# Weight loads of the -k rows issued from GpSimd's queue, those of the +k rows from SyncE's

## Chip, cores and metric

The kernel runs on one core of one Trainium2 chip. The metric is the device time of one execution in microseconds (us); lower is better. "Before" is the kernel without the change, "after" the kernel with it. Each execution is marked fast or slow: slow when it took over 1.5% longer than the fastest of the same kernel. Medians are over all executions.

## The reference

Two spectral filters work on the same input, and a gate mixes their results:

```python
x = A_x                                            # 1 x 2048 x 1024, bf16
g = sigmoid((x * gate_w).sum(-1, keepdims=True))
def branch(w_r, w_i):                              # w_r, w_i: 2048 x 513, bf16
    return irfft2(rfft2(x.astype(float32)) * (w_r + 1j * w_i), s=(2048, 1024)).astype(bfloat16)
a, b = branch(A_w_r, A_w_i), branch(B_w_r, B_w_i)
return g * a + (1 - g) * b
```

The weights are two groups, A and B, each of 2 x 2048 rows of 513 numbers: 1026 bytes a row, 4.2 MB a group. The +k rows are one half of each group, the -k rows the half that mirrors it in frequency.

## The kernel before

The transforms are matrix products on TensorE (PE), which leave their results in a buffer, PSUM. The other data lie in an on-chip memory of 128 rows, called partitions. ScalarE (ACT) and VectorE (DVE) copy the results out of PSUM, and VectorE also multiplies the spectrum by the weights. SyncE (SP) issues the loads (DMAs) in its own queue; GpSimd (POOL) has nearly nothing to do. A small scheduler in the kernel keeps each engine's operations in program order and works out the waits from keys that each operation says it reads or writes.

```python
def op(self, eng, fns, reads=(), writes=(), dma=False):
    ...
    for k in reads:
        o.deps |= self.writer[k]            # wait for who wrote it
    for k in writes:
        o.deps |= self.writer.get(k, set())   # wait for the earlier writer
        o.deps |= self.readers.get(k, set())  # and for everybody who reads it
    for k in reads:
        self.readers.setdefault(k, set()).add(o)
    for k in writes:
        self.writer[k] = {o}
        self.readers[k] = set()
    ...

def dma(eng, pairs, reads, writes, kind=True):
    S.op(eng, [lambda e, d=d, s=s: e.dma_start(d, s) for d, s in pairs], reads, writes, dma=kind)
```

The weight loads. `R5` holds group A, and `R2` holds group B. Partition 0 of `R2` first serves the gate, under the keys `zrow` and `gwt`:

```python
def wload(b):
    prs = []
    T = WR[b]; P = pit[id(T)]
    for pm in range(2):                       # +k rows, then -k rows
        for ii in range(4):
            for c in range(2):                # real, imaginary
                src = wsrc[b][c]; n = src.shape[-1]
                def part(r0, step, k0, k1):   # partitions 4*pm + ii, + 8, + 16, ...
                    prs.append((AP(T, (4*pm + ii)*P + (2*k0 + c)*NS, [[8*P, 16], [2*NS, k1-k0], [1, n]]),
                                AP(src.tensor, src.offset + r0*n, [[128*n, 16], [step*n, k1-k0], [1, n]])))
                ...
    dma("sp", prs, [], [("W", b)] + (["zrow", "gwt"] if b else []))
wload(0)
...                                           # wload(1) follows later, after stage_d(0)
```

`prod` is VectorE's product. `stage_i1` starts the inverse transform, and its copy out of PSUM writes `V` into `R1`, the buffer in which the input `x` lay (`allx` is the list of the 16 keys of `x`):

```python
def prod(b, m):
    r = [("X", 2*m), ("X", 2*m + 1), ("W", b)]          # two spectrum tiles and the weights
    dve(1230, tt(...), r, ["t0"])
    ...
def stage_i1(b, kg):
    ...
    w = [("V", b, kg)]
    if kg == 0:
        w += allx if b == 0 else [("W", 0)]
    ev(1024, ap(VR[b], kg*8, ...), pslot(s, 0, ...), [("ps", s)], w)
```

## Time and profile before

| | before |
|---|---|
| time | 163.45 us median of 2 runs (162.85 to 164.06) |
| profiled span | 159.0 us |
| PE, DVE, ACT busy | 78%, 76%, 77% |
| group A landed | 44.49 us (completion of its semaphore in the trace) |
| group B landed | 68.46 us |

The first line of the page gives busy time and share of the span; the chain line tells what the longest chain of waits ran through.

```profile
PE 124.6 (78%) x1015; PEld 90.0 (57%) x1024; DVE 120.4 (76%) x193; ACT 121.7 (77%) x132; POOL 0.2 (0%) x4
...
ACT 37%; PE 27%; DVE 22%; issue 7%; DMA 4%; SPq 1%; DVEq 0%
PE PS L313 27%; ACT R L302 21%; ACT RING L302 13%; DVE RING L316 12%; DVE R L316 6%; DMA R<-in_A_x_dram 4%; DVE RING L304 4%; ACT GROW L564 1%; ACT L564 1%; ACT V L302 1%; SPq L319 1%; DVEq L213 0%
```

No engine is full, so the chain has to be read stage by stage. This is the list of waits (who waited for whom: total us, times, longest us):

```profile
ACT R L302 <- PE PS L313: 20.9, 17, 5.1
...
DVE RING L316 <- DMA R<-in_A_w_i_dram: 10.2, 1, 10.2
```

VectorE stood 10.2 us for the weights of group A. Its timeline (start us, length us, what, elements, count, idle before and what ended it) shows when:

```profile
34.20 0.17 DVE L316 TENSOR_TENSOR ZG<-PS,GS 128x16 bf16<-128x16 f32 x1 [6.77 <-PE PS L313]
44.59 2.36 DVE L316 TENSOR_TENSOR RING<-R 128x2048 bf16<-128x2048 bf16 x2 [10.21 <-DMA R<-in_A_w_i_dram]
```

PE used up the work that it could do without that product, and then stood too; its next group of matmuls comes 3.1 us late. The profile found no releaser and calls it issue; these `KI` matmuls read the product, and VectorE's adds for it end at 48.2 us (46.87 + 1.29 in its timeline).

```profile
44.32 0.84 PE L313 MATMUL PS<-RING,S 128*128 128x512 bf16 x5 [0.34 <-ACT RING L302]
48.25 1.03 PE L313 MATMUL PS<-KI,RING 128*128 128x256 bf16 x8 [3.10 <-issue]
...
50.91 1.03 PE L313 MATMUL PS<-KI,RING 128*128 128x256 bf16 x8
...
54.62 1.04 PE L313 MATMUL PS<-DM,R 128*128 128x256 bf16 x8
```

How fast the weights came is in the windows view (stretch, its length, busy us of each engine with its number of instructions, granted TensorE clock, DMA share, GB/s):

```profile
22.00:32.00 10.00, 7.74 (x70) 4.28 (x70) 5.36 (x9) 8.35 (x10) 0.00 (x0) 1.00 1.14 171
```

The rate is 171 GB/s with the DMA engines full, while the page's slices show over 400 for the loads of `x` just before.

### The profile page before, as it was taken

The numbers are of one execution on the slowest core, as the hardware profiler recorded it, in microseconds if no ns is written. First come the engines' busy times: TensorE is split into PE (matmuls) and PEld (weight loads), VectorE is DVE, ScalarE is ACT, GpSimd is POOL, SyncE is SP. The second block draws the span as 40 slices with busy tenths as digits, with TensorE's granted clock in tenths as the row PEclk, the third lists the DMA queues.
The fourth block names the chain that finished last, engine by engine and source line by source line (L and its number), as shares of the span: only waits on it lengthen the run. The fifth ranks groups of instructions, "written<-read, shape, count | busy, mean of one in ns | idle before, by whom it ended". The sixth has DMA issues, their size and how long they took to land.

```text
span 159.0 us, 2541 instructions
## 1 busy us (share of the span) xinstructions
PE 124.6 (78%) x1015; PEld 90.0 (57%) x1024; DVE 120.4 (76%) x193; ACT 121.7 (77%) x132; POOL 0.2 (0%) x4
## 2 busy tenths in 40 slices
PE   0255897888928999999954999959999899898930
PEld 0244654355616767776633788847778576565600
DVE  0699998000079997998999999969923788989892
ACT  3045889629985988989955599999999499888850
POOL 0000000000000000000000000000000000000000
PEclk9999999999999999999995599999999999999995
DMA  5899999999999999950000000000000034243333
GB/s 168 296 429 415 257 168 167 177 167 165 179 168 170 181 169 169 197 191 4 0 0 0 0 5 0 0 0 4 0 0 1 4 112 152 86 180 123 145 132 132
DMA packets 13165, 19.53 MB, mean 123 GB/s; under 512 B 1505, under 2 KB 9825, under 8 KB 12770
## 3 DMA queue, kind: packets, MB, share of 16 engines
q1 hardware_dynamic: 13008, 19.37, 53.5%
q8 instruction: 8, 0.13, 0.4%
q14 instruction: 3, 0.02, 0.1%
q10 hardware_dynamic: 146, 0.00, 0.0%
HBM read 15.17 MB, written 4.19 MB: 122 GB/s over the span
## 4 chain that ended last, share of the span: by engine, by line
ACT 37%; PE 27%; DVE 22%; issue 7%; DMA 4%; SPq 1%; DVEq 0%
PE PS L313 27%; ACT R L302 21%; ACT RING L302 13%; DVE RING L316 12%; DVE R L316 6%; DMA R<-in_A_x_dram 4%; DVE RING L304 4%; ACT GROW L564 1%; ACT L564 1%; ACT V L302 1%; SPq L319 1%; DVEq L213 0%
## 5 line engine op out<-in xcount | busy, mean ns | idle before, releaser
L302 ACT ACTIVATE R<-PS 128x1024 bf16<-128x1024 f32 (+1 forms) x80 | 75.9, 1041 | 20.9 <-PE PS L313 20.9
L316 DVE TENSOR_TENSOR RING<-R 128x2048 bf16<-128x2048 bf16 (+1 forms) x48 | 48.0, 1041 | 16.9 <-DMA R<-in_A_w_i_dram 10.2
L302 ACT ACTIVATE RING<-PS 128x1024 bf16<-128x1024 f32 x40 | 42.8, 1135 | 8.0 <-PE PS L313 6.8
L316 DVE TENSOR_TENSOR RING<-RING 128x512 bf16<-128x512 bf16 (+1 forms) x96 | 44.6, 509 | 2.5 <-ACT RING L302 1.4
L313 PE MATMUL PS<-KI,RING 128*128 128x256 bf16 x256 | 34.0, 281 | 7.5 <-issue 3.1
L313 PE MATMUL PS<-DI,R 128*128 128x256 bf16 x256 | 32.7, 273 | 1.5 <-DVE RING L304 1.2
L313 PEld LDWEIGHTS PS<-KI,RING 128*128 128x128 bf16 x256 | 24.3, 101 | 14.0 <-issue 3.9
L313 PEld LDWEIGHTS PS<-DI,R 128*128 128x128 bf16 x256 | 24.4, 98 | 8.4 <-DVE RING L304 2.2
L313 PE MATMUL PS<-FM,R 128*128 128x128 bf16 x128 | 11.8, 266 | 13.0 <-DVE R L316 13.0
L313 PEld LDWEIGHTS PS<-FM,R 128*128 128x128 bf16 x128 | 10.1, 122 | 14.8 <-DVE R L316 14.4
L313 PE MATMUL PS<-RING,S 128*128 128x1 bf16 (+2 forms) x91 | 15.8, 304 | 1.3 <-ACT RING L302 1.1
L313 PE MATMUL PS<-DM,R 128*128 128x256 bf16 x128 | 16.4, 273 | 0.2 <-DVE RING L304 0.2
L313 PEld LDWEIGHTS PS<-DM,R 128*128 128x128 bf16 x128 | 12.0, 98 | 2.5 <-DVE RING L304 0.5
L313 PEld LDWEIGHTS PS<-RING,S 128*128 128x128 bf16 x96 | 7.8, 97 | 7.7 <-ACT RING L302 1.4
L304 DVE CAST RING<-PS 128x1024 bf16<-128x1024 f32 x8 | 10.0, 1251 | 1.9 <-PE PS L313 1.9
L316 DVE TENSOR_TENSOR R<-RING 128x1024 bf16<-128x1024 bf16 x16 | 10.3, 688 | 0.3
L313 PE MATMUL PS<-R,FM 128*128 128x512 bf16 x30 | 9.1, 379 | 1.3 <-DVE RING L304 1.3
L313 PE MATMUL PS<-RING,DM 128*128 128x512 bf16 x30 | 9.1, 379 | 0.1
L313 PE MATMUL PS<-R,G 128*1 128x512 bf16 x32 | 7.5, 378 | 0.7 <-ACT R L302 0.7
L304 DVE CAST R<-PS 128x1024 bf16<-128x1024 f32 x4 | 4.9, 1223 | 3.1 <-PE PS L313 3.1
L316 DVE TENSOR_TENSOR ZG<-PS,GS 128x16 bf16<-128x16 f32 x1 | 0.2, 175 | 6.8 <-PE PS L313 6.8
L313 PEld LDWEIGHTS PS<-RING,DM 128*128 128x128 bf16 x32 | 3.1, 98 | 3.8
(25 smaller groups left out, 26.9 us busy)
## 6 DMA issues: line engine op xcount, KB each, us to landing
out_dram<-RING SPq DMA_DIRECT2D x16, 256.0 KB, 2.0
R<-in_A_x_dram SPq DMA_DIRECT2D x3, 1024.0 KB, 10.5
R<-in_A_w_r_dram SPq DMA_DIRECT2D x7, 256.5 KB, 13.9
R<-in_A_w_i_dram SPq DMA_DIRECT2D x7, 256.5 KB, 14.7
R<-in_B_w_r_dram SPq DMA_DIRECT2D x7, 256.5 KB, 14.4
R<-in_B_w_i_dram SPq DMA_DIRECT2D x7, 256.5 KB, 14.1
R<-in_A_x_dram SPq DMA_DIRECT2D x2, 512.0 KB, 5.0
FM<-c_F SPq DMA_DIRECT2D x1, 512.0 KB, 5.0
```

The costliest lines, as they stand in the source:

```text
L302: S.op("act", lambda e: e.activation(outap, inap, ACT.Copy), reads, writes)
L304: S.op("dve", lambda e: e.tensor_copy(outap, inap), reads, writes)
L313: return lambda e: e.matmul(o, l, r, start=start, stop=stop, skip_group_check=True)
L316: return lambda e: e.tensor_tensor(out=o, in0=a, in1=b, op=op)
L319: S.op(eng, [lambda e, d=d, s=s: e.dma_start(d, s) for d, s in pairs], reads, writes, dma=kind)
L564: S.op("act", lambda e: e.activation(ap(GROW, 0, [[1, 512]]), misc(7, 0, [[1, 512]]), ACT.Sigmoid), ["m7"], ["GROW"])
```

## The change

The intent is to take the two halves of a group's rows over two queues at the same time. SyncE keeps the +k rows. GpSimd, idle so far, gets the -k rows; its loads name `("x", 15)` as read, so that they begin only when the last piece of `x` has landed.

```diff
     def wload(b):
-        prs = []
+        both = ([], [])
...
-        for pm in range(2):
-            for ii in range(4):
-                for c in range(2):
+        for ii in range(4):
+            for c in range(2):
+                for pm in range(2):
                     src = wsrc[b][c]
                     n = src.shape[-1]
+                    prs = both[pm]
...
-        dma("sp", prs, [], [("W", b)] + (["zrow", "gwt"] if b else []))
+        dma("sp", both[0], [], [("W", b, 0)] + (["zrow", "gwt"] if b else []))
+        dma("pool", both[1], [("x", 15)], [("W", b, 1)] + (["zrow", "gwt"] if b else []))
...                      # in prod, p512 and stage_i1, ("W", b) becomes ("W", b, 0), ("W", b, 1)
```

More of the change, by code (lines that the diff above doesn't have):

```diff
@@ L457, in prod @@
         ws = ap(T, 2 * m * 2 * NS + NS, [[2 * NS, 2], [-NS, 2], [1, 512]])
-        r = [("X", 2 * m), ("X", 2 * m + 1), ("W", b)]
+        r = [("X", 2 * m), ("X", 2 * m + 1), ("W", b, 0), ("W", b, 1)]
         p = PO + m % 2 * 2048
@@ L480, in stage_i1 @@
         if kg == 0:
-            w += allx if b == 0 else [("W", 0)]
+            w += allx if b == 0 else [("W", 0, 0), ("W", 0, 1)]
         ev(1024, ap(VR[b], kg * 8, [[128, 128], [1, 8]]), pslot(s, 0, [[8, 128], [1, 8]]), [("ps", s)], w)
@@ L491, in p512 @@
         ws = ap(T, NS + 512, [[-NS, 2], [2 * NS, 16]])
-        r = ["X5", ("W", b)]
+        r = ["X5", ("W", b, 0), ("W", b, 1)]
         dve(100, tt(ap(P5, o, [[16, 2], [1, 16]]), x, w, ALU.mult), r, [("p5", b, 0)])
```

## The prediction

> **What bounds the kernel now.** No single engine: over the 159.0 us span PE, DVE and ACT are each busy 76 to 78%, and the chain of waits runs through ACT (37%), PE (27%) and DVE (22%). One place hangs on the weight loads. In the waits, VectorE stands 10.2 us (34.4 to 44.6 us) for the DMA of `A_w_i`; the semaphore of the first weight group completes at 44.49 us. In the timeline PE then has nothing left it may do and stands 3.1 us (45.1 to 48.25) until the first product leaves VectorE. From 48 to 82 us DVE and PE are each busy 31.7 of 34 us, so lost time is not made up.
>
> **Why the loads are slow.** The windows show 167 to 172 GB/s at full DMA busy from 18 to 66 us, against over 400 GB/s for the `x` loads. The 1026 B packets took 47 ns each at first (17.0 to 17.5 us) and about 106 ns (median) from 18 us. The Trainium skill, "SBUF — State Buffer", section "Door 1: The DMA port swizzle", gives the port of each partition. The +k rows go to partitions whose number mod 8 is 0 to 3: 8 of 16 ports, so two engines share a port, and two times 47 ns is close to 106. The -k rows use the other 8. Today all +k loads go first, so half the ports idle. This is inferred.
>
> **The change.** It adds and removes no bytes and no compute. Of each group's 18 DMAs, 8 (+k) stay on SyncE and 10 (-k) go to GpSimd, from about 15.6 us, when the last `x` load lands. With both sets of ports in use the rate should rise to between 220 and 300 GB/s unless GpSimd's descriptor generation is slower. The skill's "DMA: Bandwidth & Descriptors" ("Rules for kernel authors") says that spreading over queues gives no bandwidth; I think the ports make this case an exception. The 2.1 MB of -k rows must land by about 41.4 us to cost no time: 2.6 us for each of ten DMAs. I expect the group complete at 34 to 40 us.
>
> **How much is on the critical path.** Not 10.2 us. The first product also needs the second spectrum tile, which ACT finishes at 40.75 us. I replayed the order of operations with the trace's durations and the weights earlier: the whole rest moves up 3.05 us, and no more however early they land; landing at 43 us gives 1.5, at 46 us loses 1.5. The second group (68.5 us now, wanted at 79) has slack to about 80 us.
>
> **Predicted time.** 163.45 - 3.05 = 160.4, plus a little for the chance that GpSimd is slow: 160.7 us, range 159.3 to 165. Faster by over 2% (below 160.2) 0.27, within 2% 0.58, slower by over 2% 0.15.
>
> **What would show each step.** Right: weight-phase rate over 220 GB/s and 1026 B packets nearer 50 to 80 ns; VectorE's first product starting at about 41.4 us, its earlier wait ended by ACT, not DMA; PE's 3.1 us gap gone. Wrong on ports: rate still about 170 GB/s, time unchanged.
>
> **What would make it wrong.** GpSimd emitting slower than 2.6 us a DMA, or held while VectorE runs its folds to 27.4 us: then the -k half starts late, lands after 44.5 us, and each us late costs one; landing after 48 us would be a loss of over 2%. Also the second group's GpSimd half landing after 80 us. Also the TensorE clock's drop (0.50 at 84 to 90 us) growing.

## The result

After: 181.97 us median of 2 runs (180.98 to 182.96), against 163.45 us. The ratio is 1.1158, 95% interval 1.0956 to 1.1359. Here and below a ratio is the one which compares the fast runs of the two kernels; it is not quite the ratio of the medians (here 1.113). The order of instructions on PE, VectorE and ScalarE is the same in both kernels.

| | before | after |
|---|---|---|
| profiled span | 159.0 us | 181.1 us |
| group A landed (SyncE half, GpSimd half) | 44.49 us, whole | 41.24 us, 38.50 us |
| VectorE's first product | 44.59 us | 41.36 us |
| group B landed (SyncE half, GpSimd half) | 68.46 us, whole | 53.65 us, 69.12 us |
| ScalarE writes the first `V` | 49.32 us | 69.20 us |

The same lines of the page of after:

```profile
PE 129.4 (71%) x1015; PEld 91.9 (51%) x1024; DVE 120.6 (67%) x193; ACT 121.6 (67%) x132; POOL 11.3 (6%) x24
...
ACT 31%; PE 27%; DMA 17%; DVE 13%; issue 5%; SPq 3%; POOL 2%; POOLq 0%; DVEq 0%; ACTq 0%
PE PS L313 27%; ACT R L302 20%; DMA R<-in_B_w_i_dram 14%; ACT RING L302 8%; DVE RING L316 7%; DMA R<-in_A_x_dram 4%; DVE R L316 3%; SPq L319 3%; DVE RING L304 3%; POOL R L319 2%; ACT GROW L566 1%; ACT L566 1%; ACT V L302 1%; POOLq L213 0%; DVEq L213 0%
```

The chain now holds 14% of loads of `in_B_w_i`, that is group B. The first part of the change worked. The rate while both queues ran was 221 GB/s instead of 171:

```profile
22.00:32.00 10.00, 8.95 (x86) 5.09 (x85) 5.36 (x9) 8.86 (x11) 0.00 (x0) 1.00 1.07 221
```

VectorE's first product came 3.2 us earlier (its wait is still ended by the load), and PE's gap of 3.1 us was gone: its `KI` matmuls follow at 45.22 us without a wait.

```profile
34.39 0.17 DVE L316 TENSOR_TENSOR ZG<-PS,GS 128x16 bf16<-128x16 f32 x1 [6.96 <-PE PS L313]
41.36 2.36 DVE L316 TENSOR_TENSOR RING<-R 128x2048 bf16<-128x2048 bf16 x2 [6.80 <-DMA R<-in_A_w_i_dram]
...
72.28 1.29 DVE L316 TENSOR_TENSOR RING<-RING 128x1024 bf16<-128x1024 bf16 x2 [20.04 <-PE PS L313]
```

```profile
44.52 0.84 PE L313 MATMUL PS<-RING,S 128*128 128x512 bf16 x5 [0.35 <-DVE RING L316]
45.22 1.03 PE L313 MATMUL PS<-KI,RING 128*128 128x256 bf16 x8
...
47.26 1.06 PE L313 MATMUL PS<-RING,S 128*128 128x512 bf16 x6
70.28 1.89 PE L313 MATMUL PS<-KI,RING 128*128 128x256 bf16 x8 [21.96 <-ACT R L302]
...
76.73 1.04 PE L313 MATMUL PS<-DM,R 128*128 128x256 bf16 x8
```

But at 47 us ScalarE stops for 22 us, PE at 48 us, and VectorE at 52 us. The waits say who stands and for what:

```profile
POOL R L319 <- DMA R<-in_B_w_i_dram: 32.5, 1, 32.5
...
ACT R L302 <- DMA R<-in_B_w_i_dram: 22.0, 1, 22.0
...
DVE RING L316 <- PE PS L313: 20.3, 2, 20.0
...
DVE RING L316 <- DMA R<-in_A_w_i_dram: 6.8, 1, 6.8
```

ScalarE's timeline before and after, at the same instruction:

```profile
45.88 1.10 ACT L302 ACTIVATE R<-PS 128x1024 bf16<-128x1024 f32 x1
49.32 1.02 ACT L302 ACTIVATE R<-PS 128x1024 bf16<-128x1024 f32 x1 [2.35 <-PE PS L313]
```

```profile
46.09 1.10 ACT L302 ACTIVATE R<-PS 128x1024 bf16<-128x1024 f32 x1
69.20 1.02 ACT L302 ACTIVATE R<-PS 128x1024 bf16<-128x1024 f32 x1 [22.01 <-DMA R<-in_B_w_i_dram]
```

This instruction copies the first `V` from PSUM into the old `x` buffer. It needs no weights of group B. Nevertheless it is held until they have landed, and VectorE and PE stand behind it. The chain between 38 and 75 us, in order of time (start us, length us, what), tells why the landing was so late:

```profile
38.94 14.71 DMA R<-in_B_w_i_dram
53.65 0.28 issue
53.93 4.41 POOL R L319 x8
...
58.91 10.21 DMA R<-in_B_w_i_dram
...
69.20 1.03 ACT R L302
```

GpSimd issues its half of group B only at 53.93 us, when SyncE's half has landed. Both waits come from the bookkeeping, not from the data:

1. The GpSimd half of group B names `("x", 15)` as read, like that of group A. A DMA counts as a reader until it has landed. The first `V` writes all keys of `x`, so it waits for every reader, and so for the landing of group B's weights, which touch neither `x` nor `V`.
2. Both halves of group B name `zrow` and `gwt` as written. The second writer of a key waits for the first, so GpSimd's half waits for SyncE's to land. Yet the -k rows go to partitions 4 to 7 of each eight, and the gate's data lie in partition 0.

The 22.1 us of span (181.1 against 159.0) add up. They are more than the 18.5 us between the medians, because the profiled execution of before was quicker than the two timed ones: later, a span of 159.1 us of before went with a time of 160.61 us. PE's second group of `KI` matmuls starts at 70.28 us instead of 50.91, which is 19.4 us later. From there to the end before took 159.0 - 50.9 = 108.1 us and after 181.1 - 70.3 = 110.8 us: 2.7 us more. All of it has arisen by the `DM` matmuls at 54.62 us before and 76.73 us after: 3.71 us against 6.45 us for the same work. In that stretch the granted TensorE clock of after was 0.50, as it had been from about 52 us on, in the standstill; before had 1.00 from 50 to 56 us.

The window of after:

```profile
70.00:76.00 6.00, 5.72 (x25) 3.52 (x26) 1.29 (x2) 4.11 (x5) 0.00 (x0) 0.50 0.00 0
```

### The profile page after: what moved, and what is told of

The parts are those of the page before. It is cut to its first block, busy times and chain, and to the rows that moved or that the text cites. A ratio compares the mean times of both kernels' runs of the same rounds, so it can differ in the third digit from the quotient of the medians.

```text
span 181.1 us, 2542 instructions
## 1 busy us (share of the span) xinstructions
PE 129.4 (71%) x1015; PEld 91.9 (51%) x1024; DVE 120.6 (67%) x193; ACT 121.6 (67%) x132; POOL 11.3 (6%) x24
## 4 chain that ended last, share of the span: by engine, by line
ACT 31%; PE 27%; DMA 17%; DVE 13%; issue 5%; SPq 3%; POOL 2%; POOLq 0%; DVEq 0%; ACTq 0%
PE PS L313 27%; ACT R L302 20%; DMA R<-in_B_w_i_dram 14%; ACT RING L302 8%; DVE RING L316 7%; DMA R<-in_A_x_dram 4%; DVE R L316 3%; SPq L319 3%; DVE RING L304 3%; POOL R L319 2%; ACT GROW L566 1%; ACT L566 1%; ACT V L302 1%; POOLq L213 0%; DVEq L213 0%
## 5 line engine op out<-in xcount | busy, mean ns | idle before, releaser
L313 PE MATMUL PS<-KI,RING 128*128 128x256 bf16 x256 | 35.9, 291 | 26.4 <-ACT R L302 24.1
L313 PEld LDWEIGHTS PS<-KI,RING 128*128 128x128 bf16 x256 | 25.3, 104 | 33.7 <-ACT R L302 25.2
L313 PE MATMUL PS<-RING,S 128*128 128x1 bf16 (+2 forms) x91 | 16.7, 315 | 1.3 <-ACT RING L302 0.8
L313 PE MATMUL PS<-DM,R 128*128 128x256 bf16 x128 | 17.3, 282 | 0.1
L313 PE MATMUL PS<-R,G 128*1 128x512 bf16 x32 | 8.8, 423 | 0.7 <-ACT R L302 0.7
L313 PEld LDWEIGHTS PS<-R,G 128*1 128x1 bf16 x32 | 2.6, 90 | 5.8 <-issue 2.0
```

Of the source, the lines that this page charges most:

```text
L313: return lambda e: e.matmul(o, l, r, start=start, stop=stop, skip_group_check=True)
```

## The experiments

Theory A: the loss comes from the two false dependencies of group B alone, and the split of the loads by itself is a gain. Rival B: GpSimd's descriptors, or the second queue's traffic, cost the time. On the smaller question why the split is quicker, the port theory (two queues write to different ports; a port is an entrance to the on-chip memory for loads, and the prediction names the map that gives each partition its port) stands against "a second queue is quicker in itself". Twelve runs of ten kernels were made (e1 to e8 and the two repeats gave correct results; e9 and e10 are wrong), each beside the kernel before on the same chip. On those chips before had medians of 161.2 to 162.5 us, so the ratios are what to compare. The intervals of e1, e3, e4, e7, e9 and e10 all lie below 1; that the gain is over 2% is clear only in e4_again.

### e1_no_reader: the false reader taken away

```diff
-        dma("pool", both[1], [("x", 15)], [("W", b, 1)] + (["zrow", "gwt"] if b else []))
+        dma("pool", both[1], [] if b else [("x", 15)], [("W", b, 1)] + (["zrow", "gwt"] if b else []))
```

> Only the bookkeeping entry changes: the second group's GpSimd half is no longer noted as a reader of the last x piece, so the first write of V into the old x buffer no longer has to wait for it. It is still issued late, after the SyncE half of its group. Theory A (two false dependencies turned a late but harmless load into a wait): the second group still lands at about 69 us, ACT's 22 us wait is gone, and the replay of the order of operations gives 3.05 us less than before, 160.4 us (ratio to before 0.981). Rival B (the loss is GpSimd's descriptors or the transfers themselves being slow or in the way): the times of landing are the same, so about 182 us, ratio 1.11.

Measured: 158.63 us median of 6 runs against 162.01; ratio 0.9792 (0.9745 to 0.9839). Group B's GpSimd half still landed at 69.18 us. ScalarE's waits from 30 to 100 us in this run:

```profile
ACT R L302 <- PE PS L313: 7.4, 9, 2.0
ACT RING L302 <- PE PS L313: 2.8, 4, 1.6
ACT V L302 <- PE PS L313: 1.7, 3, 0.7
```

ScalarE has no wait for a DMA left. Every half of a group landed within about a microsecond of its time in after. One entry in a list is worth 24.9 us of span (181.1 against 156.2), and rival B falls.

### e2_no_order and e3_neither: the false order taken away, alone and together with the reader

```diff
+        sp_half = dma("sp", both[0], ...)          # dma now returns its operation
+        gp_half = dma("pool", both[1], [("x", 15)], [("W", b, 1)] + (["zrow", "gwt"] if b else []))
+        if b:
+            gp_half.deps |= sp_half.deps
+            gp_half.deps.discard(sp_half)
```

In e3_neither the list of reads is `[] if b else [("x", 15)]` as well.

> The GpSimd half of the second group waits for the same reads of the shared buffer as the SyncE half, but no longer for the SyncE half to land; it is still noted as a reader of x. Theory A: both halves are issued from about 34.4 us. GpSimd's 4104 B packets then take most of each engine's turns (in the changed kernel 165 to 179 GB/s against 50 for SyncE), and the first group's SyncE half, not yet finished, is held up: it lands at about 48 us instead of 41.2, and the second group's GpSimd half at about 48 us. The replay then gives about 3.5 us more than before: 166 to 168 us. Rival A2 (no hold-up: the first group lands at 41.2 us as in the changed kernel, so the false reader alone costs the time to about 48 us): 163 to 164 us. Rival B: about 182 us.

> Both false dependencies away. Naively this should be the best of all. Theory A with the hold-up of the first group's SyncE half: the same as with the order alone removed, 166 to 168 us, that is slower than the version that keeps the late issue (160.4). Rival A2 (no hold-up): 160.4 us, the same as with the reader alone removed. Rival B: about 182 us.

Measured: e2 166.98 us, ratio 1.0251 (1.0166 to 1.0336); e3 158.48 us, ratio 0.9779 (0.9722 to 0.9835).

The waits of ScalarE in e2, in the same view:

```profile
ACT R L302 <- PE PS L313: 7.8, 8, 2.0
ACT R L302 <- DMA R<-in_B_w_i_dram: 7.5, 1, 7.5
ACT RING L302 <- PE PS L313: 3.3, 4, 1.6
ACT V L302 <- PE PS L313: 1.7, 3, 0.7
```

The number for e2 was met for the wrong reason. I expected group A to be held up by GpSimd's loads of group B. It was not: it landed at 41.27 us in e2 and at 40.77 us in e3. GpSimd issued from 34.6 to 40.0 us in e3, but its first bytes moved only at 38.9 us, when SyncE's old loads were nearly through. So the expectation for e3 was missed, and its rival A2 held. (A2's 163 to 164 us for e2 was missed too, because GpSimd's half of group B landed at 54.97 us and not at 48.) The loss of e2 is the false reader alone: with the earlier landing (54.97 us instead of 69.12) ScalarE's wait shrinks from 22.0 to 7.5 us but does not go. The order costs nothing by itself, as e1 against e3 shows; it only made the wait for the false reader 14 us longer.

### e4_first_only and e5_second_only: half of the change each

In e4 group B goes whole through SyncE; in e5 group A does, and group B is split as in the change.

```diff
-        dma("sp", both[0], [], [("W", b, 0)] + (["zrow", "gwt"] if b else []))
-        dma("pool", both[1], [("x", 15)], [("W", b, 1)] + (["zrow", "gwt"] if b else []))
+        if b:          # e4
+            dma("sp", both[0] + both[1], [], [("W", b, 0), ("W", b, 1), "zrow", "gwt"])
+        else:
+            dma("sp", both[0], [], [("W", b, 0)])
+            dma("pool", both[1], [("x", 15)], [("W", b, 1)])
...
+        if b:          # e5
+            dma("sp", both[0], [], [("W", b, 0), "zrow", "gwt"])
+            dma("pool", both[1], [("x", 15)], [("W", b, 1), "zrow", "gwt"])
+        else:
+            dma("sp", both[0] + both[1], [], [("W", b, 0), ("W", b, 1)])
```

> Only the first group is split over the two queues; the second goes whole through SyncE as before. Theory A: the first group lands at about 41.2 us, the second at about 66 us, no wait of ACT for it, 160.4 us (ratio 0.981), the same as with the reader removed. Rival B (GpSimd's share of the first group is what costs): clearly above 163 us.

> The first group goes whole through SyncE as before and lands at about 44.5 us; only the second group is split, with both false dependencies. Theory A (all the loss lies in the second group's dependencies): its SyncE half lands at about 57 us, its GpSimd half is issued only then and lands at about 72 us, ACT's first write of V waits for it some 22 us, and the replay gives 22.5 us more than before: about 185 us. Rival B (the loss comes with the first group's use of GpSimd): about the time of before, 162 us.

Measured: e4 158.14 us, ratio 0.9771 (0.9725 to 0.9818). e5 185.13 us of 2 runs, ratio 1.1485 (1.1392 to 1.1578), with this wait:

```profile
ACT R L302 <- DMA R<-in_B_w_i_dram: 25.0, 1, 25.0
```

The gain lies in group A and the loss in group B, as theory A says. (e5 is slower than after: behind a whole group A on SyncE's queue, GpSimd's half of group B landed at 72.32 us, and the gain of group A was missing, which landed at 45.40 us.)

### e6_same_ports and e7_one_queue: which part of the split brings the rate

e6 is e1 with `prs = both[c]` and the loop over `pm` outermost: the queues share real and imaginary parts and both begin on the +k rows. e7 has no GpSimd loads: one list in the order of the change's loops (+k and -k in turn), all on SyncE.

```diff
-        for ii in range(4):              # e6, against e1
-            for c in range(2):
-                for pm in range(2):
-                    prs = both[pm]
+        for pm in range(2):
+            for ii in range(4):
+                for c in range(2):
+                    prs = both[c]
...
-        both = ([], [])                  # e7, against e1
+        one = []
+        both = (one, one)
...
-        dma("sp", both[0], ...)
-        dma("pool", both[1], ...)
+        dma("sp", one, [], [("W", b, 0), ("W", b, 1)] + (["zrow", "gwt"] if b else []))
```

> As the version without the false reader, but the queues split real from imaginary parts, so that both carry the +k rows first and the -k rows then, on the same 8 ports at the same time. Port theory: two queues bring nothing, the rate from 22 to 32 us stays at 165 to 175 GB/s (222 with the split by ports), the first group lands at 43 to 45 us and the time is that of before, 161 to 163 us. Rival (a second queue, or its larger packets, bring the rate whatever the ports): 220 GB/s, landing at 41 us, 158.6 us.

> No GpSimd at all: all 18 loads of a group on SyncE, +k and -k loads in turn. Port theory in its strong form (only the mix of ports counts, the engines drift apart): over 220 GB/s from 22 to 32 us, first group at or before 36 us, 158.5 us. Port theory with engines in step (each engine works its queue in order, so two engines of one port meet on the same load): 165 to 175 GB/s, landing at 44 us, the time of before, 162 us. I hold the second for likelier, 60 to 40.

Measured: e6 160.86 us, ratio 0.993 (0.9854 to 1.0005), group A landed at 43.99 us. e7 158.00 us, ratio 0.9817 (0.9757 to 0.9876), group A landed at 40.96 us. In e6 SyncE's queue passed from +k to -k rows at 26.2 us and GpSimd's at 29.7 us (by the bytes of each queue), so its three windows are: both on +k rows, on different ports, both on -k rows. Below it stands the window of e7.

```profile
22.00:26.00 4.00, 3.81 (x42) 2.27 (x39) 3.96 (x7) 4.00 (x6) 0.00 (x0) 1.00 1.10 176
26.20:29.70 3.50, 2.68 (x32) 1.75 (x30) 1.29 (x2) 3.50 (x5) 0.00 (x0) 1.00 1.07 202
30.00:34.00 4.00, 2.65 (x23) 0.93 (x22) 0.00 (x0) 1.31 (x3) 0.00 (x0) 1.00 1.08 180
```

```profile
22.00:32.00 10.00, 8.36 (x82) 4.75 (x80) 5.43 (x9) 8.76 (x11) 0.00 (x0) 1.00 1.13 199
```

While both queues of e6 worked on the same ports the rate was 176 and 180 GB/s, little over the 171 of one queue; while they were on different ports it was 202. (My expectation overlooked that stretch: over 22 to 32 us the mean is 188, above the 165 to 175 expected, and the median time was 0.1 us below the range, 0.7 us if its one slow execution is left out.) So a second queue in itself brings a few per cent of rate, against 25 to 29% with the ports split (171 to 221 in after, 214 to 219 in e1 to e4, from 22 to 32 us), and the time of e6 is that of before within the noise. In e7 one queue with the loads in turn reached 199 GB/s, between my two forecasts, which was just enough to land in time. Why it is 199 and not more is open. The order of the list does most of what the second queue was meant to do for this kernel's time.

### e8_act_queue: the second queue on ScalarE

e8 is e1 with the -k loads of group A issued from ScalarE, placed after the fold of rows 8 and 9. Group B is as in e1.

```diff
+        if n2 == 8:
+            dma("act", minus_rows, [("x", 15)], [("W", 0, 1)])   # minus_rows: both[1] of group A
```

> The first group's -k rows go out on ScalarE's queue instead of GpSimd's, from about 20 us, so that both queues carry packets of 1026 B; the second group as in the version without the false reader. Theory of turns (the engines take the queues in turn, packet by packet, and GpSimd's 4104 B packets took four of five parts of the bytes, leaving SyncE's ports underused): now the bytes split evenly, 280 to 340 GB/s while both run, the first group lands by 35 us. Rival (222 GB/s is the limit of two queues or of the engines for such rows): about 222 GB/s, landing after 38 us. The time is not the point: ScalarE pays 10 issues of at least 0.6 us, so 158 to 163 us.

Measured: 167.11 us of 2 runs, ratio 1.0367 (1.0289 to 1.0445). It tells nothing about turns between equal packets: ScalarE issued from 21.83 us, but its first weight bytes moved only at 28.65 us, when SyncE's half was nearly through, so the queues hardly ran together. ScalarE itself stood 9.7 us at the issues, which is enough for what e8 lost against e1 (8.5 us by the medians). Both misses are mine; how two queues with equal packets share stays open.

### e9_wide_rows and e10_all_ports: does an even earlier landing pay?

Both are e7 with wrong contents of group A: the same bytes in wide rows. e9 writes 32.8 KB rows to 64 partitions a load, e10 16.4 KB rows to 128.

```diff
+        if b == 0:      # e10; e9 has AP(T, 64*c*P, [[P, 64], [1, 16416]]) and source rows of 16416
+            one[:] = [(AP(T, 8208*c, [[P, 128], [1, 8208]]), AP(wsrc[0][c].tensor, wsrc[0][c].offset, [[8208, 128], [1, 8208]]))
+                      for c in range(2)]
+            one += [...]   # the last 32 columns
```

> Wrong result on purpose. As the one-queue version, but the first weight group comes in as 128 wide rows of 32.8 KB instead of 4096 rows of 1026 B: the same bytes, in the wrong places, so that the group lands by about 28 us instead of 41. It tests the step of the prediction that an earlier landing than about 41.4 us is worth nothing. If ScalarE's second spectrum tile at about 40.8 us is the limit from there on: VectorE's first product still starts at 40.9 to 41.5 us and the time is that of the one-queue version within noise, 157 to 159 us, ratio to before 0.975 to 0.985. If the weights were still the limit: 12 us or so less, or at least clearly under 156 us.

> Wrong result on purpose, and the second try at an early landing: the wide rows of the try before went to 64 partitions at a time, which are only 8 ports, and landed at 40.2 us. Now each of two loads writes all 128 partitions with rows of 16.4 KB. Port theory: about twice the rate of the try before, over 350 GB/s, landing at 28 to 31 us. Then VectorE's first product is ended by ScalarE at about 40.8 us, and the time is that of the other repaired versions, 157 to 159 us, ratio to before 0.975 to 0.985: ten more microseconds of lead are worth nothing. If the weights were still a limit behind ScalarE: clearly under 156 us.

Measured: e9 158.37 us, ratio 0.9808 (0.9739 to 0.9876); e10 158.04 us, ratio 0.9772 (0.961 to 0.9934). e9 missed its aim: its 32,832 B rows took 2571 ns each (median), only a quarter less by the byte than the 1026 B rows of before (106 ns), and landed at 40.24 us. e10's 16,416 B rows took 615 ns, and landed at 29.58 us:

```profile
18.00:27.00 9.00, 8.78 (x77) 5.07 (x74) 8.86 (x15) 6.85 (x9) 0.00 (x0) 1.00 1.01 429
```

```profile
34.25 0.17 DVE L316 TENSOR_TENSOR ZG<-PS,GS 128x16 bf16<-128x16 f32 x1 [6.77 <-PE PS L313]
40.84 2.36 DVE L316 TENSOR_TENSOR RING<-R 128x2048 bf16<-128x2048 bf16 x2 [6.41 <-ACT R L302]
```

Eleven microseconds of lead over e7 brought nothing: VectorE's first product is now ended by ScalarE at 40.84 us. The pair also bears on the ports: with 16 engines, 2571 ns for 32,832 B is 204 GB/s and 615 ns for 16,416 B is 427 GB/s. In e9 a load covers partitions 0 to 63 or 64 to 127, which are 8 of the 16 ports in the map that the prediction names. The trace agrees with it: half the ports, half the rate. But e9's rows are also twice as long, and no run here separates the two; that wide rows on 8 ports stay near 200 GB/s is what the pair shows.

### e7_again and e4_again: the two best once more, five rounds

> The one-queue version again, beside the wide rows on the same chip and with more rounds, because it needs no GpSimd and no second dependency: 158 us, ratio 0.980 with an interval under one per cent wide.

> The split of the first group alone, on the same chip as the one-queue version: the same time within half a per cent, since both land the first group at about 41 us and neither has a wait for the second.

Measured on one chip: e7 158.64 us, ratio 0.981 (0.976 to 0.986); e4 157.65 us, ratio 0.9751 (0.9704 to 0.9798). e4 is 0.6% lower, a little more than I expected. Its six times, 157.34 to 158.15 us, hardly overlap those of e7, 158.02 to 159.19 us, so e4 is probably the better by a little, but the intervals of the ratios overlap. Both beat before and after.

## Why the prediction was wrong

- **The step that failed:** "The second group (68.5 us now, wanted at 79) has slack to about 80 us." That is so for the kernel before. In the changed kernel its GpSimd half was wanted at 47 us, by ScalarE's first write of `V`, because it was on the list of readers of `x`; it landed at 69.12 us, well before 80, and still cost a wait of 22.0 us. Nor was it issued beside SyncE's half: the order held it until 53.93 us. I had replayed the order of operations of before with other landing times, not the dependencies of the changed kernel. The diff shows both: `[("x", 15)]` is passed for both groups, and `zrow` and `gwt` are written twice. e1 takes away one entry and turns 1.116 into 0.979.
- **The size of the gain was right.** 3.05 us were forecast from the split. The runs without the false reader gave 3.4 (e1), 3.5 (e3) and 3.9 us (e4) by medians, and 2.8 us in the span of e1 (156.2 against 159.0). That the whole gain came was partly luck: the group landed at the limit, as the next two points tell.
- **The limit at 41.4 us was right.** e10 landed 11 us earlier than e7 for the same time, with the wait ended by ScalarE at 40.84 us. In after the first product began at 41.36 us as forecast, but its wait was ended by the load, not by ScalarE.
- **The ports were right, the landing was optimistic.** The rate was 221 GB/s in after and 214 to 219 in e1 to e4, at or just under the low end of 220 to 300; SyncE's 1026 B packets took 92 ns (median, 22 to 32 us of after), not 50 to 80; and the group was complete at 41.24 us instead of 34 to 40: just in time. GpSimd's packets are of 4104 B for most rows, SyncE's of 1026 B, and from 24 to 28 us in e1 GpSimd moved 172 GB/s and SyncE 49. The Trainium skill ("DMA: Bandwidth & Descriptors", "Queues, rings and completion order") says that an engine takes its queues in turn by packets; if the packets of the trace are meant, the measured shares, about 3.5 to 1, agree roughly with that. The skewed shares left SyncE's ports partly idle (49 GB/s, where before had 171 on the same ports); that the packet size is the cause is argued and not shown, since e8 could not test it.
- **What I feared did not happen.** GpSimd issued a load of 256 rows in 0.56 us, not 2.6, both while VectorE was busy with folds (group A) and while it stood (group B). The stall that the skill warns of ("SBUF — State Buffer", the box on DVE blocking DMA) did not show; those folds are two-input operations, for which the same page expects none. GpSimd's first weight bytes did move only 5.9 us after its first issue, but in e3 this delay was 4.4 us for group B while VectorE stood idle (34.5 to 40.9 us), so the folds are not needed for it.
- **Not forecast:** 2.7 us more while the granted TensorE clock was 0.50 for some 6 us after the standstill. (The drop that the prediction feared, at 84 to 90 us of before, is another; it did not grow, and lies at about 107 to 114 us of after.)

## What to carry to other kernels

When a load gets a new key or a new issuer, list again who must now wait for it, above all the writers of any key that it claims to read: in this bookkeeping a DMA stays a reader until it lands, and a read named only to delay an issue can hold a write far away. Before adding a queue, look at which partitions the loads in flight write; putting loads for different ports next to each other in the one queue gave most of the gain here (1.9% of 2.5% on one chip). And find what comes behind the wait: here only 3 of the 10 us were to be had.

## What the Trainium skill lacked or had wrong

- "DMA: Bandwidth & Descriptors" ("Rules for kernel authors") says that spreading loads over issuers brings no bandwidth. Here 171 GB/s became 221, because the two queues wrote to different ports; with the same ports (e6) it was 176 to 180, nearly as the page says. It lacks that the order of loads within one queue matters: +k and -k in turn gave 199 (e7).
- "SBUF — State Buffer" ("Door 1") gives its advice and bandwidths for ranges of partitions. Strided sets are caught too: rows to partitions 0 to 3 of each eight took about 106 ns for 1026 B, against 47 ns at 17.0 to 17.5 us, when they began (before).
- "DMA: Bandwidth & Descriptors" gives about 1 us to the first byte for GpSimd's loads. With SyncE's loads outstanding it was 5.9 us (issue 15.86, first packet 21.78 us, after), 4.4 us in e3 (34.55 and 38.91 us), and 1.3 us with none (53.93 and 55.20 us, after). ScalarE's queue showed 6.8 us (21.83 and 28.65 us, e8).
- The same page says that a packet of GpSimd's queue is preferably up to 4096 B ("SWDGE vs HWDGE vs iDMA"); 4104 B, four rows, were seen here. It lacks the size for SyncE's queue, here one row (1026 B), and so the warning that a turn each is not an equal share (172 against 49 GB/s).
